# A fused attention and two-layer feed-forward kernel: float64 weights are loaded into their final places and converted in four stages, and two units share one product with v

## The chip, the cores and the metric

The kernel runs on one core of a Trainium2 chip. The metric is the device time of one execution in microseconds (us), as the median of several runs. Five engines work at once: TensorE (PE; its weight loads are shown apart as PEld), VectorE (DVE), ScalarE (ACT), GpSimd (POOL) and SyncE (SP), which issues most of the DMAs. Each engine runs its own instructions strictly in the order in which the program issues them, as the traces below show.

## The reference

Three layers follow each other, in float32 on activations; the four weight matrices arrive as float64 words:

```python
scores = q @ k.T / 8                     # 4 batches, 8 heads, 576 positions, head size 64
scores = where(mask, scores, -1e9)       # 4 heads: window of 32; 4 heads: 32 positions, 4 apart
x = softmax(scores) @ v                  # then 2304 tokens x 512
h = x @ w_in ; y = (h - tanh(h)) @ w_out           # 512 -> 2048 -> 512
h2 = y @ w_in2 ; s = h2 * softmax(h2)              # 512 -> 1024
out = layernorm(s) * g_ln @ w_out2                 # 1024 -> 512
```

## The kernel before, in words

The 2304 tokens form 6 groups of 384 (`G`). A group has 8 attention units (`NU`), 48 in all; a unit is two heads on two blocks of 96 queries with 128 keys each. Of a unit, `qk_f32` (units below 22) or `qk_half` makes the scores in PSUM and the DVE masks them and takes row minima (L163, L187, L190); `sm_exp` is the exponential on ACT (L198); `sm_norm` is two small DVE instructions (L203, L204) and one product on POOL (L205); `tr_pe` transposes on TensorE (L212) and ACT copies the result to `pt` (L218); `pv_pe` multiplies by v (L233), and ACT and DVE write the rounded part and the rest of the result into `x` (L243, L244). Units from 22 on need their operands in two parts as well, which `prep_unit` writes into `qks` with three DVE instructions (L139 to L142).

Products are made with float32r operands in two parts, high and rest, so that every product of the feed-forward layers takes three passes. A weight tile of 128 x 512 float64 words is loaded raw by `w_load` (L78, 512 KB), and `w_step` turns it into its two parts, one step of the pipeline for each of several tiles at once: ACT scales the upper words (L97), the DVE takes the sign and joins the parts of the word (L98, L101, L105), and two steps later ACT casts to the high part (L85) and the DVE subtracts it (L86).

The program has four stretches. **Start**: rounds r = 0 to 10 run the 8 units of the first group, and in rounds 1 to 10 one `w_step` each (`SW`). In a round TensorE has `qk(r)`, `pv(r - 3)`, `tr(r - 2)` in this order; the DVE has first the `w_step`, then the minima of unit r, the x part of an earlier unit and the norm of unit r - 1; ACT has its part of the `w_step`, then the exponentials of unit r and the copy to `pt`. SP issues, in order, the raw load of the `w_step`, then `load_unit(r + 3)`. **Main loop**: iteration s has two halves (slots). Half 0 is `mm1(s)`, 12 passes over one tile of `w_in` for group s // 16; half 1 is `mm2(s - 5)`, 12 passes over one tile of `w_out` that add to four PSUM tiles `yb`. `todo` holds the pieces of attention that TensorE does behind the passes of a slot, `later` the work of the other engines; `plan` lays them out by slot: unit u from 16 on starts in slot p = 4u - 41. In slots 0 to 41 `w_step` is called at the pace of WA steps in WB slots. After the 16th tile of a group `mm2` copies the four `yb` through an SBUF tile `ys` to `y_dr` in DRAM (L330, L331, L332), two at a time through one buffer. **Last group** (s from 80): no attention is left; one `w_step` per iteration converts `w_in2` and `w_out2` into the 16 places of `wi`, whose old tiles are used for the last time by `mm1(80)` to `mm1(95)`. **End**: for 18 tiles of 128 tokens `mm3`, `softmax`, `trz`, `mm4`, `store`.

Of the kernel before, what the change touches and what calls it, by code (L numbers as in the profile page):

```python
# [16 lines left out]
WIN, DIL = 32, 4  # L17
# [14 lines left out]
WA, WB = 24, 40  # L32
# [5 lines left out]
def tile_kernel(ctx: ExitStack, tc: tile.TileContext, qk, vw, cst, w_in, w_out, w_in2, w_out2, g_ln, out):  # L38
# [4 lines left out]
    wi_p = ctx.enter_context(tc.tile_pool(name="wi", bufs=NF, side="left"))  # L43
    wo_p = tc.alloc_tile_pool(name="wo", bufs=NF, side="left")
    raw_p = tc.alloc_tile_pool(name="raw", bufs=3, side="left")
    qs_p = None
# [25 lines left out]
    wq, wld, wa, wf = [], [], [], []  # L72
# [8 lines left out]
    def w_parts():  # L81
        if wf:
# [6 lines left out]
    def w_step():  # L89

        w_parts()
        new = wld.pop(0) if wld else None
        if new:
            lst, c, pool, tag, nm, r = new
            a = raw_p.tile([128, 512], F32, tag="wa", name="wa_" + nm, bufs=2)
            y = raw_p.tile([128, 512], I32, tag="wy", name="wy_" + nm, bufs=3)
            nc.scalar.activation(out=a, in_=r[:, :, 1].bitcast(F32), func=AF.Copy, scale=2.0 ** -112)  # L97
            nc.vector.tensor_scalar(out=y, in0=r[:, :, 1], scalar1=-2 ** 31, scalar2=None, op0=ALU.bitwise_and)  # L98
        if wa:
            *e, ao, yo = wa.pop(0)  # L100
            nc.vector.scalar_tensor_tensor(out=yo, in0=ao.bitcast(I32), scalar=3, in1=yo,  # L101
                                           op0=ALU.logical_shift_left, op1=ALU.bitwise_or)
            wf.append((*e, yo.bitcast(F32)))
        if new:
            nc.vector.scalar_tensor_tensor(out=y, in0=r[:, :, 0], scalar=29, in1=y,  # L105
                                           op0=ALU.logical_shift_right, op1=ALU.bitwise_or)
            wa.append((lst, c, pool, tag, nm, a, y))
# [4 lines left out]
    for c in range(NF + LAG):  # L112
        if c < NF:
            wq.append((wi, c, wi_p, w_in[c], "wi", f"wi{c}"))
        if c >= LAG:
            wq.append((wo, c - LAG, wo_p, w_out[c - LAG], "wo", f"wo{c - LAG}"))
# [6 lines left out]
    def load_unit(u):  # L123
        if u < NU * NG:
# [3 lines left out]
            v = at_p.tile([NK, 2, 2, D], F32, tag="v", name=f"v{u}", bufs=4)  # L128
# [3 lines left out]
    def prep_unit(u):  # L132
# [3 lines left out]
        s = qs_p.tile([128, QC + 2 * KC], F32R, tag="qks", name=f"qks{u}")  # L136
# [71 lines left out]
    def tr_pe(u, pool, tag, eng="a"):  # L208
# [4 lines left out]
        pt = at_p.tile([NK, QC], F32, tag="pt", name=f"pt{u}")  # L213
# [9 lines left out]
    def pv_pe(u, pool, tag):  # L223
        d = un.pop(u)
        g, r = divmod(u, NU)
        hp, bp = divmod(r, 2)
        if bp == 0:
# [408 lines left out]
```

## Time and profile before

| what | us |
|---|---|
| median of 3 runs (769.83 to 771.4) | 770.56 |
| the profiled execution, its own time | 771.82 |
| its span, first to last instruction | 770.0 |
| TensorE busy in it | 729.4 |

The profile shows one execution. An instruction has a start, a duration and, in brackets, the idle time of its engine before it with what ended that. Start times are us from the start of the span. Stretches of one engine's idle time matter only where the work that ends last waits for them. "Issue" as releaser means that the profile names no cause.

### The profile page before, as it was taken

The page shows a single profiled execution, that of the slowest core. Times are in us where ns is not written, and L with a number is a line of the kernel's source. Part 1 is how long each engine was busy: PE and PEld are TensorE (multiplying, and loading weights), DVE is VectorE, ACT ScalarE, POOL GpSimd, SP SyncE. Part 2 cuts the span into 40 slices and gives each one's busy share as a digit, 9 for nine tenths or more (in the row PEclk, how much of TensorE's full clock was granted, in tenths as well). Part 3 has the DMA queues.
Part 4 walks back from the last instruction along what each step waited for, and adds up shares of the span by engine and source line. Part 5 has one row for each costly group of instructions (what it writes and reads, how often), then busy time and mean ns, then how long its engine had stood idle before and what let it go on. Part 6 is the DMA issues. An engine that isn't in the chain of part 4 may idle for free.

```text
span 770.0 us, 11751 instructions
## 1 busy us (share of the span) xinstructions
PE 729.4 (95%) x4168; PEld 657.8 (85%) x4168; DVE 470.0 (61%) x1297; ACT 367.1 (48%) x1015; POOL 132.3 (17%) x187
## 2 busy tenths in 40 slices
PE   5658899999999999999999999799999999999998
PEld 4547789999999899989998999799888888888885
DVE  4688788746665766666666535498365555555453
ACT  4656666644443544444444434345145544445454
POOL 1210322111111111111111100010133123231210
PEclk9999899999999999999999999899999999999999
DMA  7565354222222222121212102434201011110001
GB/s 188 180 215 154 110 187 162 92 70 77 63 62 78 88 63 63 62 89 55 64 61 94 63 1 82 155 133 138 68 1 56 29 40 56 42 54 28 14 28 42
DMA packets 30283, 63.62 MB, mean 83 GB/s; under 512 B 3088, under 2 KB 16912, under 8 KB 30224
## 3 DMA queue, kind: packets, MB, share of 16 engines
q1 hardware_dynamic: 26960, 58.15, 23.6%
q10 hardware_dynamic: 3264, 4.72, 1.7%
q8 instruction: 33, 0.54, 0.3%
q14 instruction: 26, 0.21, 0.1%
HBM read 53.42 MB, written 9.44 MB: 82 GB/s over the span
## 4 chain that ended last, share of the span: by engine, by line
PE 88%; DMA 4%; DVE 3%; ACT 2%; issue 1%; POOL 1%; SPq 0%; ACTq 0%; POOLq 0%; DVEq 0%
PE y L325 27%; PE h L298 25%; PE po L529 13%; PE h L467 13%; PE pv L233 3%; PE zt L510 2%; DMA raw_wi<-in_w_in_dram 2%; PE qkp L158 2%; PE tp L212 2%; PE qkp L178 2%; ACT p L198 1%; DMA y_dr<-ys 1%; POOL p L205 1%; DVE wy_wi L105 1%; DMA raw_wo<-in_w_out_dram 0%
## 5 line engine op out<-in xcount | busy, mean ns | idle before, releaser
L298 PE MATMUL h<-x,wi 128*128 128x384 f32 x1152 | 225.3, 346 | 3.3 <-DVE x L244 2.0
L325 PE MATMUL y<-gs,wo 128*128 128x384 f32 x1152 | 222.6, 343 | 4.3 <-DVE ys L330 4.3
L325 PEld LDWEIGHTS y<-gs,wo 128*128 128x128 f32 x1152 | 199.9, 190 | 9.4 <-DVE ys L330 4.6
L298 PEld LDWEIGHTS h<-x,wi 128*128 128x128 f32 x1152 | 202.0, 193 | 5.5 <-DVE x L244 2.3
L205 POOL TENSOR_TENSOR p<-p,rs 96x512 f32<-96x512 f32 x48 | 77.9, 1623 | 368.0 <-DVE rs L204 315.3
L306 ACT ACTIVATE t<-h 128x384 f32<-128x384 f32 x96 | 46.9, 489 | 125.3 <-PE h L298 119.3
L467 PE MATMUL h<-w2i,yt 128*128 128x512 f32 x432 | 104.9, 397 | 0.0
L529 PE MATMUL po<-w2o,z 128*128 128x512 f32 x432 | 104.1, 396 | 0.1
L529 PEld LDWEIGHTS po<-w2o,z 128*128 128x128 f32 x432 | 80.7, 188 | 20.4 <-ACT z L518 1.9
L518 ACT ACTIVATE z<-zt,gl_sb 128x128 fp32r<-128x128 f32 x144 | 51.0, 367 | 96.9 <-PE zt L510 48.6
L467 PEld LDWEIGHTS h<-w2i,yt 128*128 128x128 f32 x432 | 79.7, 187 | 18.4
L198 ACT ACTIVATE p<-p,nm 96x128 f32<-96x128 f32 x192 | 75.0, 393 | 36.3 <-DVE nm L163 36.3
L519 DVE SCALAR_TENSOR_TENSOR z<-zt,gl_sb,z 128x128 fp32r<-128x128 f32 x144 | 48.9, 350 | 69.2 <-ACT z L518 69.2
L312 ACT CAST gs<-t 128x384 fp32r<-128x384 f32 x96 | 49.1, 511 | 54.0 <-DVE t L309 53.7
L244 DVE TENSOR_TENSOR x<-pv,x 128x192 fp32r<-128x192 f32 x48 | 20.5, 428 | 77.1 <-ACT x L243 77.1
L309 DVE TENSOR_TENSOR t<-h,t 128x384 f32<-128x384 f32 x96 | 52.9, 551 | 23.0 <-ACT t L306 22.9
L315 DVE TENSOR_TENSOR gs<-t,gs 128x384 fp32r<-128x384 f32 x96 | 56.1, 585 | 9.8 <-ACT gs L312 9.7
L233 PE MATMUL pv<-pt,v 128*64 128x96 f32 x384 | 29.7, 281 | 15.7 <-ACT pt L218 9.1
L233 PEld LDWEIGHTS pv<-pt,v 128*64 128x64 f32 x384 | 19.8, 151 | 28.6 <-issue 12.4
L158 PE MATMUL qkp<-qkr 64*96 64x128 f32 x176 | 31.6, 334 | 8.2 <-DMA qkr<-in_qk_dram 7.6
L387 POOL TENSOR_TENSOR yt<-yr,yt 128x1024 fp32r<-128x1024 f32 x9 | 21.9, 2430 | 93.9 <-DMA raw_w2o<-in_w_out_dram 62.3
L158 PEld LDWEIGHTS qkp<-qkr 64*96 64x96 f32 x176 | 25.9, 201 | 13.0 <-DMA qkr<-in_qk_dram 6.9
(68 smaller groups left out, 708.2 us busy)
## 6 DMA issues: line engine op xcount, KB each, us to landing
qkr<-in_qk_dram SPq DMA_DIRECT2D x26, 448.0 KB, 3.4
raw_wi<-in_w_in_dram SPq DMA_DIRECT2D x16, 512.0 KB, 4.5
raw_wo<-in_w_out_dram SPq DMA_DIRECT2D x16, 512.0 KB, 4.2
v<-in_vw_dram SPq DMA_DIRECT2D x48, 128.0 KB, 2.1
qkr<-in_qk_dram SPq DMA_DIRECT2D x22, 224.0 KB, 4.3
y_dr<-ys ACTq DMA_DIRECT2D x12, 384.0 KB, 2.4
yr<-y_dr SPq DMA_DIRECT2D x9, 512.0 KB, 4.1
out_dram<-o SPq DMA_DIRECT2D x18, 256.0 KB, 2.0
```

Source lines behind the costliest of these rows:

```text
L158: nc.tensor.matmul(ps[:, b], d["r"][:64, b * NQ:(b + 1) * NQ], d["r"][:64, QC + b * NK:QC + (b + 1) * NK], start=True, stop=True)
L198: nc.scalar.activation(out=d["p"][:, b], in_=d["p"][:, b], func=AF.Exp, scale=-1.0, bias=d["nm"][:, b:b + 1], accum_out=d["sm"][:, b:b + 1])
L205: nc.gpsimd.tensor_tensor(out=d["p"], in0=d["p"], in1=d["rs"].unsqueeze(2).to_broadcast([NQ, 4, NK]), op=ALU.mult)
L233: nc.tensor.matmul(ps[64 * h:64 * h + 64, b * NQ:(b + 1) * NQ], d["v"][:, b, h], d["pt"][:, (2 * h + b) * NQ:(2 * h + b + 1) * NQ], start= ...
L298: nc.tensor.matmul(ps, w[:, a, k * 128:(k + 1) * 128], xt[g, k][:, b], start=(n == 0), stop=(n == 3 * KD - 1))
L309: nc.vector.tensor_tensor(out=t, in0=ps, in1=t, op=ALU.subtract)
L312: nc.scalar.copy(out=gs[:, 0], in_=t)
L315: nc.vector.tensor_tensor(out=gs[:, 1], in0=t, in1=gs[:, 0].bitcast(F32), op=ALU.subtract)
L325: nc.tensor.matmul(yb[g][m], wo[c][:, a, m * 128:(m + 1) * 128], gs[:, b], start=(c == 0 and i == 0), stop=(c == NF - 1 and i == 2))
L467: nc.tensor.matmul(ps[:, n * 512:(n + 1) * 512], y[:, a, k, o:o + TT], w2i[2 * k + n][:, b], start=(q == 0), stop=(q == 3 * KD - 1))
L518: nc.scalar.activation(out=z[:, 0, c], in_=pp[n][:, j], func=AF.Copy, scale=gc)
L529: nc.tensor.matmul(po, z[:, a, j], w2o[j][:, b], start=(q == 0), stop=(q == 3 * NF2 - 1))
```

## The change

- Raw tiles have no pool of their own: each raw tile is loaded into the place that its two parts take later (tags `wi0` to `wi15`, `wo0` to `wo15`, one buffer each); scratch tiles for the conversion (`cv`) are kept for the whole program. Four raw tiles are loaded ahead in the start, where it was two.
- `w_step` has four stages: the DVE's subtraction (L86 before) comes one step after ACT's cast (L85), and stands first in the step; ACT's scaling stands ahead of the cast.
- WA is 26, where it was 24.
- `pv_pe` does two units in a row into one PSUM bank, with one pair of instructions for x; in the start it runs in rounds 4, 6, 8 and 10, in the main loop for odd u. `v` has 6 buffers for 4, `pt` 3 for 2.
- `qks` has one buffer for two, and its three instructions come in slots p + 2, p + 3, p + 3 where they came in p, p + 1, p + 2.
- `ys` holds all four tiles of a group, which go out with one DMA.

```diff
-WA, WB = 24, 40
+WA, WB = 26, 40
...
-            raw = raw_p.tile([128, 1024], I32, tag="raw", name="raw_" + nm)
+            raw = pool.tile([128, 1024], I32, tag=tag, name="raw_" + nm)
             nc.sync.dma_start(out=raw, in_=src)
...
     def w_step():
-        w_parts()
+        if wh:
+            lst, c, w, f = wh.pop(0)
+            nc.vector.tensor_tensor(out=w[:, 1], in0=f, in1=w[:, 0].bitcast(F32), op=ALU.subtract)
+            lst[c] = w
...
+            nc.scalar.activation(out=a, in_=r[:, :, 1].bitcast(F32), func=AF.Copy, scale=2.0 ** -112)
+            nc.vector.tensor_scalar(out=y, in0=r[:, :, 1], scalar1=-2 ** 31, scalar2=None, op0=ALU.bitwise_and)
         if wf:
             lst, c, pool, tag, nm, f = wf.pop(0)
             w = pool.tile([128, 2, 512], F32R, tag=tag, name=nm)
             nc.scalar.copy(out=w[:, 0], in_=f)
-            nc.vector.tensor_tensor(out=w[:, 1], in0=f, in1=w[:, 0].bitcast(F32), op=ALU.subtract)
-            lst[c] = w
+            wh.append((lst, c, w, f))
...
     def pv_pe(u, pool, tag):
+        ps = pool.tile([128, 512], F32, tag=tag, name=f"pv{u}")[:, 0:G]
+        for i in range(2):
+            d = un.pop(u + i)
+            for b in range(2):
+                for h in range(2):
+                    nc.tensor.matmul(ps[64 * h:64 * h + 64, (2 * i + b) * NQ:(2 * i + b + 1) * NQ], d["v"][:, b, h],
+                                     d["pt"][:, (2 * h + b) * NQ:(2 * h + b + 1) * NQ], start=True, stop=True)
...
     load_unit(2)
-    w_load()
+    for _ in range(3):
+        w_load()
...
-        b1 = pv_pe(r - 3, st_ps, "pv") if 0 <= r - 3 < NU else None
+        b1 = pv_pe(r - 4, st_ps, "pv") if r % 2 == 0 and 0 <= r - 4 < NU else None
...
-            for i in range(0, KD, 2):
-                ys = g_p.tile([128, 2, G], F32, tag="ys", name=f"ys{g}_{i}", bufs=1)
-                nc.vector.tensor_copy(out=ys[:, 0], in_=yb[g][i])
-                nc.scalar.copy(out=ys[:, 1], in_=yb[g][i + 1])
-                nc.scalar.dma_start(out=y_dr[:, i:i + 2, g * G:(g + 1) * G], in_=ys)
+            ys = g_p.tile([128, KD, G], F32, tag="ys", name=f"ys{g}", bufs=1)
+            for m in range(KD):
+                if m % 2 == 0:
+                    nc.vector.tensor_copy(out=ys[:, m], in_=yb[g][m])
+                else:
+                    nc.scalar.copy(out=ys[:, m], in_=yb[g][m])
+            nc.scalar.dma_start(out=y_dr[:, :, g * G:(g + 1) * G], in_=ys)
...
-                at(p, lambda u=u: preps.extend(prep_unit(u + 1)))
-                for i in range(3):
+                at(p + 2, lambda u=u: preps.extend(prep_unit(u + 1)))
+                for i in (2, 3, 3):
                     at(p + i, lambda: preps.pop(0)() if preps else None)
...
-            if u0 <= u - 2 < u1:
-                piece(q + 1, lambda u=u: pv_pe(u - 2, a_ps, "at"))
+            if u % 2 and u0 <= u - 3 < u1:
+                piece(q + 1, lambda u=u: pv_pe(u - 3, a_ps, "at"))
```

## Rows read from the trace of the kernel before

**Rows 1.** The page: busy time, share of span and instructions of each engine.
```profile
PE 729.4 (95%) x4168; PEld 657.8 (85%) x4168; DVE 470.0 (61%) x1297; ACT 367.1 (48%) x1015; POOL 132.3 (17%) x187
```
**Rows 2.** Waits of TensorE, whole span: total us, times, longest us.
```profile
PE pv L233 <- ACT pt L218: 9.1, 6, 3.5
...
PE y L325 <- DVE ys L330: 4.3, 1, 4.3
PE pv L233 <- issue: 3.8, 3, 1.3
```
**Rows 3.** Stage windows: busy us (instructions) by engine, granted clock, DMA share, GB/s.
```profile
450.00:500.00 50.00, 45.74 (x256) 44.69 (x256) 23.19 (x45) 18.14 (x37) 0.00 (x0) 0.93 0.27 90
```
**Rows 4.** Timeline, one round of the start: start, duration, engine, line, operation.
```profile
16.66 0.62 ACT L85 CAST wi<-wy_wi 128x512 fp32r<-128x512 f32 x1
...
16.80 0.91 PE L233 MATMUL pv<-pt,v 128*64 128x96 f32 x8 [0.35 <-ACT pt L218]
17.30 0.69 DVE L86 TENSOR_TENSOR wi<-wy_wi,wi 128x512 fp32r<-128x512 f32 x1 [1.74 <-ACT wi L85]
...
17.64 0.90 PE L212 MATMUL tp<-cst_sb,p 96*128 96x96 f32 x4
...
18.47 2.02 PE L158 MATMUL qkp<-qkr 64*96 64x128 f32 x8
...
19.45 0.28 DVE L163 CUSTOM_DVE_ANT_0 p<-qkp,cst_sb 96x128 f32<-96x128 f32 x1
...
20.49 0.17 DVE L204 RECIPROCAL rs<-rs 96x4 f32<-96x4 f32 x1
...
21.75 0.62 ACT L85 CAST wi<-wy_wi 128x512 fp32r<-128x512 f32 x1
```
**Rows 5.** Timeline, end of the start: minima of unit 7, first product.
```profile
40.25 0.28 DVE L163 CUSTOM_DVE_ANT_0 p<-qkp,cst_sb 96x128 f32<-96x128 f32 x1
...
52.88 6.67 PE L298 MATMUL h<-x,wi 128*128 128x384 f32 x24 [2.03 <-DVE x L244]
```
**Rows 6.** Stage window in the first loads, columns as in Rows 3.
```profile
8.00:12.00 4.00, 2.36 (x12) 2.04 (x12) 2.21 (x12) 2.38 (x11) 0.26 (x1) 1.00 0.97 274
```
**Rows 7.** Timeline, POOL: the same product in the start and later.
```profile
20.81 1.04 POOL L205 TENSOR_TENSOR p<-p,rs 96x512 f32<-96x512 f32 x1 [4.06 <-ACT p L198]
...
76.49 2.85 POOL L205 TENSOR_TENSOR p<-p,rs 96x512 f32<-96x512 f32 x1 [8.21 <-DVE rs L204]
```
**Rows 8.** Waits between 53 and 112 us, columns as in Rows 2.
```profile
DVE wi L86 <- ACT wi L85: 4.7, 4, 1.2
...
PE tp L212 <- POOL p L205: 4.2, 1, 4.2
```
**Rows 9.** Timeline of TensorE in the main loop, around one pv piece.
```profile
239.28 2.33 PE L298 MATMUL h<-x,wi 128*128 128x384 f32 x12
241.54 0.55 PE L233 MATMUL pv<-pt,v 128*64 128x96 f32 x8
242.02 2.36 PE L325 MATMUL y<-gs,wo 128*128 128x384 f32 x12
244.22 0.40 PE L178 MATMUL qkp<-qks 128*96 128x256 f32 x2
```
**Rows 10.** Timeline of the DVE at the end of group 1.
```profile
251.09 0.56 DVE L330 COPY ys<-y 128x384 f32<-128x384 f32 x1 [3.04 <-DMA y_dr<-ys]
```
**Rows 11.** Timeline of TensorE at the end of group 4.
```profile
480.44 2.24 PE L298 MATMUL h<-x,wi 128*128 128x384 f32 x12
...
484.60 2.24 PE L298 MATMUL h<-x,wi 128*128 128x384 f32 x12
...
492.14 2.29 PE L325 MATMUL y<-gs,wo 128*128 128x384 f32 x6 [4.26 <-DVE ys L330]
...
500.18 2.07 PE L298 MATMUL h<-x,wi 128*128 128x384 f32 x11
```
**Rows 12.** Loads of raw_w2i, the tile's view: from issue to landing.
```profile
DMA to landing us min/median/max: 3.0/3.2/4.4
```

More of the change, by code (lines that the diff above doesn't have):

```diff
@@ L42, in tile_kernel @@
     const = ctx.enter_context(tc.tile_pool(name="const", bufs=1, side="left"))
[L43 to L46, printed above, removed]
+    cv_p = ctx.enter_context(tc.tile_pool(name="cv", bufs=2, side="left"))
+    wi_p = ctx.enter_context(tc.tile_pool(name="wi", bufs=1, side="left"))
+    wo_p = tc.alloc_tile_pool(name="wo", bufs=1, side="left")
     g_p = ctx.enter_context(tc.tile_pool(name="g", bufs=2, side="right"))
@@ L85, in w_parts @@
             nc.scalar.copy(out=w[:, 0], in_=f)
[L86 to L98 removed]
+            wh.append((lst, c, w, f))
         if wa:
[L100 removed]
+            *eo, ao, yo = wa.pop(0)
             nc.vector.scalar_tensor_tensor(out=yo, in0=ao.bitcast(I32), scalar=3, in1=yo,
                                            op0=ALU.logical_shift_left, op1=ALU.bitwise_or)
[L103 removed]
+            wf.append((*eo, yo.bitcast(F32)))
         if new:
@@ L135, in prep_unit @@
         r = un[u]["r"]
-        s = qs_p.tile([128, QC + 2 * KC], F32R, tag="qks", name=f"qks{u}")
+        s = at_p.tile([128, QC + 2 * KC], F32R, tag="qks", name=f"qks{u}", bufs=1)
         un[u]["s"] = s
@@ L223, in pv_pe @@
     def pv_pe(u, pool, tag):
[L224 removed]
         g, r = divmod(u, NU)
[L226 to L240 removed]
+        hp = r // 2
+        x = xt[g, hp] = x_p.tile([128, 2, G], F32R, tag=f"x{hp}", name=f"x{g}_{hp}")
+        ps = pool.tile([128, 512], F32, tag=tag, name=f"pv{u}")[:, 0:G]
[5 more added lines that the diff above has]
+                                     d["pt"][:, (2 * h + b) * NQ:(2 * h + b + 1) * NQ], start=True, stop=True)
+        sl, src = [x[:, i] for i in range(2)], ps
+        if hp >= 2:
+            sl = [a.rearrange("p (i r) -> p r i", r=DIL) for a in sl]
+            src = ps.rearrange("p (r i) -> p r i", r=DIL)
         def then():
@@ L371, in tile_kernel @@
     w2i, w2o = [None] * (2 * KD), [None] * NF2
-    wq2 = [(w2i, 2 * k + n, wi_p, w_in2[k, n], "wi", f"w2i{2 * k + n}") for k in range(KD) for n in range(2)]
-    wq2 += [(w2o, j, wi_p, w_out2[j], "wi", f"w2o{j}") for j in range(NF2)]
+    wq2 = [(w2i, 2 * k + n, wi_p, w_in2[k, n], f"wi{2 * k + n}", f"w2i{2 * k + n}")
+           for k in range(KD) for n in range(2)]
+    wq2 += [(w2o, j, wi_p, w_out2[j], f"wi{2 * KD + j}", f"w2o{j}") for j in range(NF2)]
     yt, y_raw = {}, {}
@@ L396, in tile_kernel @@
     for s in range(NS + LAG):
-        if s == NF + LAG:
-            assert not (wq or wld or wa or wf)
-            raw_p.release()
-            qs_p = tc.alloc_tile_pool(name="qs", bufs=2, side="left", reuse_waits="tile")
         if s == NS - NF:
-            assert not todo and not later and not (wq or wld or wa or wf), (todo, later)
+            assert not todo and not later and not (wq or wld or wa or wf or wh), (todo, later)
             a_ps.release()
             at_p.release()
-            qs_p.release()
-            raw_p = tc.alloc_tile_pool(name="raw2", bufs=2, side="left", reuse_waits="tile")
             h2a = tc.alloc_tile_pool(name="h2a", bufs=1, space=PSUM, side="right", reuse_waits="tile")
```

35 lines of the change are left out of this document (13 added, 22 removed).

## The prediction

> **What bounds the kernel now.** The page comes first: TensorE is busy for 95% of the span [rows 1]. In such a kernel only TensorE's idle time, its time at the lower clock and work taken from it can be won, so the second view is the list of TensorE's waits [rows 2]. It names three that this change touches: pv waits for the copy to pt (9.1 us, in the start), y waits once for a copy to ys (4.3 us), and pv waits three times 1.3 us for "issue". The third view, busy time by stage, adds the clock: between 450 and 500 us, where the wait for ys lies, the granted clock is 0.93 on average [rows 3]. In the start the clock reads full, but there the same pv piece takes 0.91 us and in the main loop 0.55 us [rows 4, 9], so the start runs near the lower level of 1.2 GHz. The end of the kernel is not touched; it keeps its time.
>
> **The start: the ring of a round.** Followed back by its releasers, a round is a ring of ACT and DVE: ACT's cast at 16.66, the DVE's subtraction that waited for it at 17.30, the rest of the step on the DVE, the minima at 19.45, the exponentials and the pt copy on ACT, and behind them the next cast at 21.75: 5.1 us [rows 4]. From unit 3 (19.45) to unit 7 (40.25) the minima come 20.8 us apart, 5.2 us a round [rows 4, 5]. The four-stage step opens the ring: the subtraction uses a cast of the step before, so the DVE waits for no cast of its own round. What is left is the next longest of the engines. The DVE needs 3.36 us from the subtraction to the reciprocal's end (17.30 to 20.66) and some 0.25 us for x: 3.6 us. TensorE at the lower clock needs 2.0 for qk, 0.84 for pv and 0.83 for the transposes (starts at 16.80, 17.64, 18.47): 3.7 us. I take 3.9 us, because POOL's product, which fell into the DVE's wait, now collides with the DVE (below). Four rounds: 20.8 - 15.6 = 5.2 us won.
>
> Two things take from this. Four raw tiles instead of two are queued before the units' own loads; the DMA engines are full then, 274 GB/s at a share of 0.97 [rows 6], so two more tiles of 0.52 MB hold the operands of unit 3 back by 2 x 1.9 us. Unit 3 had nearly that much slack, its minima waiting for the DVE; I charge 0.25 us, with 0 to 2 as bounds. A round moves 0.88 MB (units 0.22 + 0.13, raw 0.52), 3.2 us at that rate, below 3.9.
>
> The tail from unit 7's minima to the first product takes 12.63 us now [rows 5]. Behind the change it is this chain: minima, x and a norm 1.7 us; a step 2.15 (17.30 to 19.45); the norm of unit 7 0.36; the next step 2.15, in which POOL is shut out, then its product 1.04; transposes 0.9 and copy 0.4; pv of two units 1.8; both parts of x 1.05: 11.6 us, 1.0 won. Together the start wins 5.2 - 0.25 + 1.0 = 6.0 us; bounds 2 and 9 (the upper one if the denser work brings TensorE to 2.4 GHz and POOL is not held).
>
> POOL's product takes 1.04 us in the start, beside a DVE that waits, and 2.85 us later, beside one that works [rows 7]; that is the collision that I charge. The Trainium skill, "SBUF — State Buffer", section "SBUF: two separate sides", says that the DVE and GpSimd share a pair of ports as an exclusive lock held for a whole instruction, by DVE instructions with two SBUF inputs among others. By it the fast rows of the start hold only as long as the DVE idles there. By the row of the start alone, the tail would be 10.4 us and a round 3.7, and the whole sum 2.0 us more.
>
> **The first slots of the main loop.** Here the DVE is late: TensorE waits 4.2 us for POOL's product of one unit, which waits for the norm on the DVE, and the DVE's subtraction waits four times for the cast, 4.7 us [rows 8]. Two of these waits stand ahead of that norm. WA = 26 moves no more steps ahead of it: slots 0, 1, 3, 4, 6, 8 have one before, 0, 1, 3, 4, 6, 7 behind. So TensorE goes on by 1.2 to 2.4 us earlier, and the first pv leaves this stretch at the lower clock (0.91) and comes back at the full one (0.5). I take 2.0 us; bounds 0 (the step in slot 7 delays the minima of unit 9 as much) and 4 (the clock does not fall).
>
> **pv of two units in a row.** In the main loop TensorE has no gap, so its own time counts. Two plain products of 12 passes take 4.16 us (480.44 to 484.60), 2.08 each [rows 11]. The product ahead of a pv piece takes 2.26 (239.28 to 241.54), the piece 0.48, the product behind it 2.20 [rows 9]: a piece costs 0.78, of which 0.30 is entry and exit. A second unit in the same piece pays 0.48 again and no second entry. 20 pairs in the main loop: 20 x 0.30 = 6.0 us. From below the bound is 0, if the second unit's first weights pay the entry again; above, 6.5.
>
> The Trainium skill, "TensorE: Matmul & The Clock Gate", section "Part 2: What happens when you issue a matmul", says that TensorE pulls weight loads ahead of matmuls in flight when their rows do not conflict, or into a background buffer. Taken alone, that would leave no entry to save and this term at 0; the row shows 0.18 us at the entry. The result by it stands among the rivals.
>
> **ys with four tiles.** Now the second pair of copies waits for the first DMA, 3.04 us at the end of group 1 [rows 10]; the DVE stands still, the PSUM buffer of a piece stays full, and the next pv has its wait for "issue", three times, 3.8 us [rows 2]. At the end of group 4 the copy waits longer, and product y with it: 4.26 us, and the clock drops. From the product at 484.60 to the one two iterations later at 500.18 are 15.58 us, where two iterations take 8.32: 7.26 us lost [rows 11]. With four tiles no copy waits for a DMA of its own group; the DMA before it is a whole group old. The last copy ends half a microsecond behind the product, and nobody needs the bank before the next `mm2`. Won: 3.8 + 7.3 = 11.1 us; lower bound 8.1, if a part of the clock's fall comes back.
>
> **What I cost at nothing.** Weights are ready one step later; the pace pays for it (`wi[15]` needs step 28, 30 are done; `wo[10]` step 29, 31 are done). The raw loads of `w_in2` and `w_out2` get a new wait: place k is free only behind `mm1(80 + k)`. Queued behind it on SP are the later raw loads and the loads of y; ACT's scaling and the DVE's step of the next iteration wait for it, and behind these the rest of tanh's work. A load lands in 3.2 us, at most 4.4 [rows 12]; then scaling, cast, high part and tanh(s + 1) on ACT and the DVE's subtraction end some 2.8 us later (five instructions of 0.5 to 0.6), 6.0 to 7.2 us behind `mm1(s)`. The PSUM buffer that this frees is wanted by `mm1(s + 3)`, five products or 10.4 us behind it. The cover is 3 to 4 us; if it is gone, each of 16 iterations grows by the excess. `qks` with one buffer: the first of three DVE instructions comes a slot behind the last reader, and they end a slot before TensorE needs them; cover some 3 us. Longer v and pt chains wait on older buffers only.
>
> **Sum.** 6.0 + 2.0 + 6.0 + 11.1 = 25.1 us. The profiled execution's own time of 771.82 becomes 746.7; it lies 1.3 above the median, so the median becomes 745.5, rounded 746.
>
> **Rivals.** (1) The loads rule the start: the operands of unit 3 come 2 us late and rounds stay at 4.8 us, so that the start wins 0.6 instead of 6.0: 751. For it speaks the full DMA [rows 6], against it that four prefetched tiles leave the queue only the mean rate to keep. (2) A pair pays its entry twice: 752. (3) The new wait of the raw loads spreads: beside the y loads they land after 8 us, beyond the cover, and 16 iterations grow by 0.5 to 1 us: 754 to 762. (4) Slower: the single `qks` stops TensorE in each of 25 units, because the DVE is late with it by more than its cover of 3 us. From 1.0 us a unit on, the whole gain of 25.1 us is gone; at 1.5 us the time is 783. Against it speaks that the DVE is idle for 39% of the span [rows 1]. (5) The chain of the ys copies just moves: the loads of y and the single larger DMA let TensorE wait as before, and 7.3 us are not won: 753.
>
> **How the numbers follow.** Forecast 0.60; rivals: (1) 0.13, (2) 0.12, (3) 0.04, (4) 0.04, (5) 0.04; several of them at once 0.03, of which 0.02 would end within 0.2%. All upper bounds of the terms at once win 5.5 us more, half of the way to all lower bounds loses 7.5 us: 740 to 753. The range of 739 to 756 adds (1), (2), (5) and part of (3), and leaves out (4) and the ends. Changes below 0.2%, 1.5 us, can't be told from none here. Faster 0.94, same 0.02, slower 0.04.
>
> **What would show it.** In the profile behind the change: minima of units 3 to 7 some 3.9 us apart and the first product near 47 us; no wait of y for ys and no pv that waits for "issue"; a pv piece of 16 matmuls near 0.96 us with one entry; clock 1.0 between 450 and 500 us; ACT and the DVE idle for raw_w2i once an iteration without a wait of TensorE. A first product later than 50 us, a second entry inside a pair, or TensorE waiting for qks would make the prediction wrong.

## The result, and the profile after

| | before | after |
|---|---|---|
| median of the runs (lowest to highest) | 770.47 us (769.83 to 771.4) | 746.64 us (746.35 to 747.18) |
| the profiled execution, its own time | 771.82 | 747.18 |
| its span | 770.0 | 745.4 |
| TensorE busy in it | 729.4 | 717.0 |

The ratio is 0.9691, with a 95% interval of 0.9674 to 0.9707: 23.8 us are won, where 25.1 were forecast. The first view of after is again the list of TensorE's waits (total, times, longest, in us).

```profile
PE qkp L158 <- DMA qkr<-in_qk_dram: 11.2, 4, 4.4
PE tp L212 <- POOL p L205: 5.4, 6, 2.3
PE qkp L158 <- DVE nm L163: 3.8, 2, 3.6
PE h L297 <- DVE x L242: 1.8, 1, 1.8
PE qkp L178 <- DVE qks L142: 0.8, 3, 0.3
```

The three waits of [rows 2] are gone, down to one of 0.5 us for pv. What stands there now lies mostly in the start and the first slots: operands from DRAM, GpSimd's product, the minima. Only the `qks` line, three small waits, belongs to the main loop.

The timeline of after gives the landmarks of the start: the minima of units 3 and 7, and the first product.

```profile
20.17 0.29 DVE L163 CUSTOM_DVE_ANT_0 p<-qkp,cst_sb 96x128 f32<-96x128 f32 x1 [2.32 <-PE qkp L158]
...
35.21 0.29 DVE L163 CUSTOM_DVE_ANT_0 p<-qkp,cst_sb 96x128 f32<-96x128 f32 x1 [0.70 <-PE qkp L158]
...
47.42 6.69 PE L297 MATMUL h<-x,wi 128*128 128x384 f32 x24 [1.83 <-DVE x L242]
```

Four rounds take 15.04 us, 3.76 each, against 20.8 in [rows 4, 5]. In the first slots behind it one wait is left, and the matmuls behind it run at the lower clock (4.04 us for 12 passes):

```profile
67.23 2.02 PE L158 MATMUL qkp<-qkr 64*96 64x128 f32 x8 [3.62 <-DVE nm L163]
69.17 4.04 PE L297 MATMUL h<-x,wi 128*128 128x384 f32 x12
```

In the main loop a piece holds both units' products with v, 16 matmuls:

```profile
228.07 2.33 PE L297 MATMUL h<-x,wi 128*128 128x384 f32 x12
230.33 0.88 PE L233 MATMUL pv<-pt,v 128*64 128x96 f32 x16
231.14 2.35 PE L324 MATMUL y<-gs,wo 128*128 128x384 f32 x12
...
308.08 0.88 PE L233 MATMUL pv<-pt,v 128*64 128x96 f32 x16
327.88 0.88 PE L233 MATMUL pv<-pt,v 128*64 128x96 f32 x16
```

The window from 450 to 500 us, where [rows 3] had a busy time of 45.74 and a clock of 0.93, has no gap at all now:

```profile
450.00:500.00 50.00, 50.00 (x290) 50.00 (x289) 39.09 (x72) 23.85 (x48) 4.65 (x1) 1.00 0.50 164
```

Two more landmarks are the DVE's first copy to `ys` and the first `mm3`, here before and after:

```profile
167.82 0.56 DVE L330 COPY ys<-y 128x384 f32<-128x384 f32 x1 [1.88 <-PE y L325]
...
548.02 11.36 PE L467 MATMUL h<-w2i,yt 128*128 128x512 f32 x48
```

```profile
158.53 0.56 DVE L330 COPY ys<-y 128x384 f32<-128x384 f32 x1 [1.88 <-PE y L324]
...
522.94 11.36 PE L462 MATMUL h<-w2i,yt 128*128 128x512 f32 x48
```

Set side by side, the landmarks say where the time went. The first product comes 5.46 us earlier (52.88 to 47.42), the DVE's first copy to `ys` 9.29 (167.82 to 158.53), the first `mm3` 25.08 (548.02 to 522.94). The end, which the change leaves alone, takes 222.5 us instead of 222.0, so that the span is 24.6 us shorter. The medians differ by 23.8 because the profiled execution of before lies 1.35 us above its median, that of after 0.54.

### The profile page after: what moved, and what is told of

Same layout as the page of the kernel before. It is cut to its first block, busy times and chain, and to the rows that moved or that the text cites. A ratio compares the mean times of both kernels' runs of the same rounds, so it can differ in the third digit from the quotient of the medians.

```text
span 745.4 us, 11617 instructions
## 1 busy us (share of the span) xinstructions
PE 717.0 (96%) x4168; PEld 653.4 (88%) x4168; DVE 490.8 (66%) x1273; ACT 365.5 (49%) x991; POOL 134.7 (18%) x187
## 4 chain that ended last, share of the span: by engine, by line
PE 88%; DVE 5%; ACT 3%; DMA 2%; POOL 1%; issue 1%; ACTq 0%; SPq 0%; POOLq 0%; DVEq 0%
PE y L324 26%; PE h L297 24%; PE po L524 14%; PE h L462 14%; PE qkp L158 3%; PE pv L233 2%; PE zt L505 2%; PE tp L212 2%; DMA qkr<-in_qk_dram 2%; PE qkp L178 2%; ACT p L198 1%; POOL p L205 1%; DVE gs L314 1%; DVE wi L85 1%; DVE p L163 1%
## 5 line engine op out<-in xcount | busy, mean ns | idle before, releaser
L324 PE MATMUL y<-gs,wo 128*128 128x384 f32 x1152 | 217.3, 338 | 0.0
L314 DVE TENSOR_TENSOR gs<-t,gs 128x384 fp32r<-128x384 f32 x96 | 75.7, 788 | 20.9 <-ACT gs L311 18.8
L158 PE MATMUL qkp<-qkr 64*96 64x128 f32 x176 | 32.5, 340 | 15.6 <-DMA qkr<-in_qk_dram 11.2
L242 DVE TENSOR_TENSOR x<-pv,x 128x384 fp32r<-128x384 f32 x24 | 16.9, 703 | 40.0 <-ACT x L241 40.0
L389 POOL TENSOR_TENSOR yt<-yr,yt 128x1024 fp32r<-128x1024 f32 x9 | 24.3, 2697 | 85.8 <-DVE yt L388 85.8
L479 DVE SCALAR_TENSOR_TENSOR u<-h,e 128x1024 f32<-128x1024 f32 x18 | 22.0, 1225 | 23.9 <-ACT e L478 23.9
L198 ACT ACTIVATION_READ_ACCUMULATOR p<-p,nm 96x1 f32 x192 | 36.2, 188 | 0.0
```

The source lines that it names most:

```text
L158: nc.tensor.matmul(ps[:, b], d["r"][:64, b * NQ:(b + 1) * NQ], d["r"][:64, QC + b * NK:QC + (b + 1) * NK], start=True, stop=True)
L198: nc.scalar.activation(out=d["p"][:, b], in_=d["p"][:, b], func=AF.Exp, scale=-1.0, bias=d["nm"][:, b:b + 1], accum_out=d["sm"][:, b:b + 1])
L314: nc.vector.tensor_tensor(out=gs[:, 1], in0=t, in1=gs[:, 0].bitcast(F32), op=ALU.subtract)
L324: nc.tensor.matmul(yb[g][m], wo[c][:, a, m * 128:(m + 1) * 128], gs[:, b], start=(c == 0 and i == 0), stop=(c == NF - 1 and i == 2))
```

## The experiments

All kernels were timed against the kernel before on the same chip. Unless another is named, each starts from the changed kernel and alters one thing. Prices are differences of medians to the 746.64 us above. The kernel before came out at 769.26 to 771.29 us in the four comparisons, so a difference of 1 us across two of them shows nothing. No run takes back by itself the pace WA, the pairs of the start, the places of the raw tiles or the single `qks` buffer.

### Undoing one part at a time

**Cast and subtraction in one step again.** ACT's cast is moved from the third stage to just ahead of the DVE's subtraction, as in the kernel before.

```diff
+        if wf:
+            lst, c, pool, tag, nm, f = wf.pop(0)
+            w = pool.tile([128, 2, 512], F32R, tag=tag, name=nm)
+            nc.scalar.copy(out=w[:, 0], in_=f)
+            wh.append((lst, c, w, f))
         if wh:
             lst, c, w, f = wh.pop(0)
...
-        if wf:
...
```

> The changed kernel with one thing undone: the DVE's subtraction stands again in the step of ACT's cast, behind it; loads, places, pace and pairs stay as changed. Theory (the ring of ACT and DVE set the round): minima of units 3 to 7 again some 5.1 us apart instead of 3.8, the first product at 52 to 53 us instead of 47.4, a time of 752 to 754 us. Rival (the loads ahead and the separate places shortened the start): rounds stay below 4.2 us, the first product before 49 us, a time below 748.5 us.

754.85 us (754.37 to 755.37), 8.2 above the changed kernel and a little above the 752 to 754 expected. Its DVE timeline shows the ring again: the subtraction waits 1.74 us for the cast, and the minima of successive units come 5.1 us apart.

```profile
23.16 0.69 DVE L90 TENSOR_TENSOR wi<-wy_wi,wi 128x512 fp32r<-128x512 f32 x1 [1.73 <-ACT wi L86]
...
25.31 0.28 DVE L163 CUSTOM_DVE_ANT_0 p<-qkp,cst_sb 96x128 f32<-96x128 f32 x1
...
28.25 0.69 DVE L90 TENSOR_TENSOR wi<-wy_wi,wi 128x512 fp32r<-128x512 f32 x1 [1.74 <-ACT wi L86]
...
30.40 0.28 DVE L163 CUSTOM_DVE_ANT_0 p<-qkp,cst_sb 96x128 f32<-96x128 f32 x1
```

The first product is at 52.74, back at the place of [rows 5] (52.88) although four tiles are still loaded ahead and pv still goes in pairs. So without the fourth stage nothing of the gain in the start is left. The stretch from the first product to the first copy of `ys` grows as well, from 111.1 to 113.6 us: 2.5 us of the first slots hang on the same wait.

**One unit per piece in the main loop.** `pv_one` is `pv_pe` of the kernel before; the start keeps its pairs.

```diff
-            if u % 2 and u0 <= u - 3 < u1:
-                piece(q + 1, lambda u=u: pv_pe(u - 3, a_ps, "at"))
+            if u0 <= u - 2 < u1:
+                piece(q + 1, lambda u=u: pv_one(u - 2, a_ps, "at"))
```

> The changed kernel with pv done unit by unit in the main loop, as before; the start keeps its pairs. Theory (a pair pays entry and exit of a pv piece once): 20 pairs lose 0.3 to 0.4 us each, 752.6 to 754.6 us, and two units take 19.7 us on TensorE in the main loop instead of 19.3. Rival (the pair costs TensorE what two single pieces cost): 746 to 747.5 us.

752.77 us (752.37 to 752.89), 6.1 more: 0.31 us for each of 20 pairs. TensorE's timeline has a piece every 9.85 us:

```profile
223.63 0.55 PE L233 MATMUL pv<-pt,v 128*64 128x96 f32 x8
...
233.48 0.55 PE L233 MATMUL pv<-pt,v 128*64 128x96 f32 x8
```

Two units take 19.70 us here and 19.32 in the changed kernel, 0.38 less. Between the landmarks the price is smaller: from the first product to the first `mm3` this execution takes 480.66 us, two executions of the changed kernel 475.52 and 475.05. The list of waits of this kernel has no `qks` line, though `qks` has one buffer here too.

**Two tiles of `ys` at a time again**, the code of the kernel before in `mm2`.

```diff
-            ys = g_p.tile([128, KD, G], F32, tag="ys", name=f"ys{g}", bufs=1)
...
+            for i in range(0, KD, 2):
+                ys = g_p.tile([128, 2, G], F32, tag="ys", name=f"ys{g}_{i}", bufs=1)
...
```

> The changed kernel with ys for two tiles and two DMAs per group through one buffer, as before. Theory (both kinds of waits at group ends came from ys): three waits of 1.3 us at the ends of groups 1 to 3 and 4.3 us with the fall of the clock at the end of group 4 come back, 757 to 758 us. Rival (the pairs already removed the three short waits, since behind the end of a group there is no pv piece any more in the next slot): only 7.3 us come back, 753.5 to 754.5 us, and TensorE has one wait for ys in its list.

758.64 us (757.98 to 759.1), 12.0 more. The waits are back, at two places (list of waits):

```profile
PE qkp L178 <- DVE qks L142: 6.8, 3, 2.3
...
PE y L324 <- DVE ys L329: 1.9, 1, 1.9
```

The DVE stands 3.02 us in front of the second copy, for the first DMA, as in [rows 10]. But TensorE now pays for it in the scores, not in pv: with one buffer, `qks` is late by 2.3 us at the end of a group. In the kernel before the same delay cost 1.3 us each [rows 2]. The wait is not all of it: behind two of the three waits the clock falls (granted 0.57 from 244 to 248 us). From one pv piece to the next the three ends of groups take 23.34, 23.39 and 21.79 us where other pairs take 19.32, 10.6 us in all; in the kernel before they took 11.2 us where other pieces take 9.86, 4.0 in all. At the end of group 4 it is the other way round: the wait of y is 1.9 us here against 4.26 in [rows 11], and from the last pv piece to the first `mm3` this kernel loses 3.75 us against the changed one (83.71 to 79.96), where [rows 11] lost 7.3. The time lies near the theory's 757 to 758, but its parts are others.

The three prices add up to 26.3 us, 2.5 more than the whole change wins. They are not shares of the gain: with the single `qks` buffer, two tiles of `ys` cost 6.5 us more at the ends of groups than in the kernel before, and 3.5 us less at the end of group 4.

### The wait that the change brought in the first slots

**The steps of the main loop later by 9/26 of a slot** (the expectations call it a quarter), so that the step of slot 7 falls into slot 8 and no longer stands ahead of unit 9's minima.

```diff
-            if s < NF + LAG and done[0] < W0 + WA * (slot + 1) // WB or s > NS - NF and half == 0:
+            if s < NF + LAG and done[0] < W0 + (WA * (slot + 1) - 9) // WB or s > NS - NF and half == 0:
```

> The changed kernel with the pace of the weight steps shifted, so that a step that fell into slot 7 of the main loop falls into slot 8, behind the minima of unit 9. Theory (that step is what makes TensorE wait 3.6 us for these minima, and the wait brings the lower clock for the next two pieces): the wait falls below 1.5 us, the clock stays at 1.0 between 60 and 75 us, a time of 741 to 743.5 us. Rival (the DVE has too much to do in these slots wherever the step stands): the wait comes back one or two slots later, 745.5 to 747.5 us.

745.93 us (745.35 to 746.37), a ratio of 0.9689 against 0.9691: no difference that can be told. TensorE's timeline shows why.

```profile
65.84 1.11 PE L158 MATMUL qkp<-qkr 64*96 64x128 f32 x8 [1.47 <-DVE nm L163]
66.89 3.75 PE L297 MATMUL h<-x,wi 128*128 128x384 f32 x12
...
72.33 0.55 PE L212 MATMUL tp<-cst_sb,p 96*128 96x96 f32 x4 [1.69 <-POOL p L205]
```

The wait for the minima shrinks from 3.62 to 1.47 us, and a wait of 1.69 us for the next unit's norm appears, by way of GpSimd. The clock does not stay at 1.0 as the theory had it: the product behind the shorter wait takes 3.75 us, and 0.87 is granted from 60 to 70 us. The DVE is busy for 9.88 of these 10 us. Moving its work by a slot renames a good part of the wait, but not all: from the first product to the first copy of `ys` this execution takes 109.01 us, two executions of the changed kernel 111.11 and 110.72. In the time, the later first product (48.19) hides some of these 2 us.

### GpSimd's product, the loads and the tail of the start

The start of the same code does not repeat exactly: in five executions with the changed kernel's start the first product came at 46.18, 47.42, 47.58, 47.79 and 48.19 us, and the minima of unit 3 between 18.88 and 20.22. A shift below 1 us at that place shows nothing by itself. The tail behind the minima of unit 7 repeats: 12.20 or 12.21 us in all five.

**The norm ahead of the minima**, in the start.

```diff
+        if r >= NU and r - 1 < NU:
+            sm_norm(r - 1)
         if r in SW:
             w_step()
+        if 0 <= r - 1 < NU - 1:
+            sm_norm(r - 1)
         if t:
             t()
...
-        if 0 <= r - 1 < NU:
-            sm_norm(r - 1)
```

> The changed kernel with one order altered in the start: on the DVE, the norm of unit r-1 (1e-9 added, reciprocal) stands ahead of the minima of unit r instead of behind them, and for the last unit ahead of the step. In the changed kernel GpSimd's product takes 2.85 us in six of the eight rounds of the start, beside the step's subtraction and its bit operations on the DVE; in the kernel before it took 1.04, beside a DVE that waited. Theory (the step's instructions hold GpSimd back): a product that begins ahead of the minima has them and the DVE's wait for TensorE beside it, so most products fall to 1.0 to 1.6 us, TensorE's waits for GpSimd in the start (1.39 and 2.35 us at 39.96 and 43.21) shrink to less than half, the first product comes 1.5 to 2.5 us earlier (45 to 46 instead of 47.4), and the time is about 744.5. Rival (the length comes from something else, such as GpSimd's own start or the full DMA): the products stay at 2.85 us, the norm waits for the exponentials and delays the minima, a round grows from 3.76 to 4 us or more, and the time is 747 to 749.

745.5 us (745.24 to 746.61), ratio 0.9668 (0.9654 to 0.9683). GpSimd's timelines, first of the changed kernel, then of this one:

```profile
29.31 2.85 POOL L205 TENSOR_TENSOR p<-p,rs 96x512 f32<-96x512 f32 x1 [1.66 <-ACT p L198]
32.56 2.85 POOL L205 TENSOR_TENSOR p<-p,rs 96x512 f32<-96x512 f32 x1 [0.41 <-ACT p L198]
```

```profile
30.40 1.04 POOL L205 TENSOR_TENSOR p<-p,rs 96x512 f32<-96x512 f32 x1 [3.39 <-DVE rs L204]
33.98 1.03 POOL L205 TENSOR_TENSOR p<-p,rs 96x512 f32<-96x512 f32 x1 [2.54 <-DVE rs L204]
36.41 4.99 POOL L205 TENSOR_TENSOR p<-p,rs 96x512 f32<-96x512 f32 x1 [1.40 <-DVE rs L204]
```

Seven products fall to 1.04 us. The eighth, which now begins beside the first instruction of a step and has a second step right behind that one, takes 4.99 us. It ends 0.98 us after the DVE has turned to an x that it reads from PSUM (40.42):

```profile
36.16 0.66 DVE L85 TENSOR_TENSOR wi<-wy_wi,wi 128x512 fp32r<-128x512 f32 x1
36.74 0.42 DVE L93 TENSOR_SCALAR wy_wi<-raw_wi 128x512 int32<-128x512 int32 x1
...
39.82 0.68 DVE L105 SCALAR_TENSOR_TENSOR wy_wo<-raw_wo,wy_wo 128x512 int32<-128x512 int32 x1
40.42 0.84 DVE L242 TENSOR_TENSOR x<-pv,x 128x384 fp32r<-128x384 f32 x1
```

The length was the DVE's doing: the theory holds on that. On the time it does not: a round shrinks only from 3.76 to 3.72 us (3.77 to 4.01 in the four other executions of the unchanged start) and the tail from 12.21 to 11.92, and the intervals of the two ratios overlap. The first product comes at 45.65, as expected, but one execution of the unchanged start had it at 46.18. GpSimd was hardly on the path of a round.

**Two raw tiles ahead instead of four.**

```diff
-    for _ in range(3):
-        w_load()
+    w_load()
```

> The changed kernel with two raw tiles loaded ahead of the units' own loads instead of four, as in the kernel before. In the changed kernel TensorE waits for the operands of unit 3 until 18.04 us, and the first minima that follow the new pace are at 20.17, 0.7 later than the same ones in the kernel before (19.45); the charge for this in the prediction was 0.25 us, with 0 to 2 as bounds. Theory (the two extra tiles of 0.52 MB stand ahead of these operands in the queue, at 1.9 us each): the operands come 2 to 3.5 us earlier, the minima of unit 3 near 18.5, and the first product 0.5 to 1.5 us earlier, because the later steps then wait for their raw tiles for a part of it: 745 to 746. Rival (the DMA engines are full whatever the order, and what is taken from the operands goes to the steps): the steps wait for their raw tiles from the second on, rounds grow from 3.76 to over 4 us, and the first product comes at 47.5 to 50: 747 to 749.

745.84 us (745.12 to 746.38), ratio 0.9671 (0.9654 to 0.9687). The minima of unit 3 come at 18.46 as expected, those of unit 7 at 34.09, 3.91 us a round, and the first product at 45.96. Of 1.7 us at unit 3 against the changed kernel's profile, 1.1 are left at unit 7. But one of the five executions with four tiles had these minima at 18.88, so that the two tiles cost between 0.4 and 1.8 us there, and in the time nothing can be told from it.

**The last two products on the DVE.**

```diff
-        nc.gpsimd.tensor_tensor(out=d["p"], in0=d["p"],
+        (nc.vector if u in (NU - 2, NU - 1) else nc.gpsimd).tensor_tensor(out=d["p"], in0=d["p"],
```

> The changed kernel with the normalizing product of units 6 and 7 on the DVE instead of GpSimd; the other units stay. It measures what the tail of the start pays for GpSimd being held: in the changed kernel the tail from the minima of unit 7 to the first product takes 12.21 us, where 11.6 were charged with 1.04 us for this product and 10.4 was the figure without any holding. Theory (TensorE's two waits for GpSimd, 1.39 and 2.35 us, lie on the chain that sets the first product): the product takes some 0.7 us on the DVE, the transposes of unit 7 start near 41 instead of 43.21, and the first product comes 1.8 to 2.5 us earlier, near 45.2, a tail of 10.0 to 10.4; the time is about 744.5. Rival (the DVE sets the chain anyway, as its queue holds both parts of x and two steps): the first product comes less than 0.7 us earlier and the time stays at 746 to 747.

746.42 us (746.06 to 747.38), ratio 0.968 (0.9665 to 0.9694). The theory falls: the tail is 11.41 us (34.98 to 46.39), not 10.0 to 10.4. The first product comes 1.0 us earlier than in the changed kernel's profile, between theory and rival, and the time is the rival's. TensorE gets its transposes sooner and then waits longer for x, 3.35 us instead of 1.83:

```profile
46.39 7.08 PE L297 MATMUL h<-x,wi 128*128 128x384 f32 x24 [3.35 <-DVE x L242]
```

### Three edits at once, and what bounds the first 80 us

**The norm ahead of the minima, two tiles ahead, the steps of the main loop later**, all three.

> The changed kernel with three edits of earlier runs at once: the norm ahead of the minima in the start, two raw tiles loaded ahead instead of four, and every step of the main loop a quarter of a slot later. Alone they moved the span by -2.0, -1.6 and -1.4 us. Theory (up to some 80 us the DVE is the bound, so what one edit wins ahead of it is partly given back as a wait for minima or norms there): the first product comes near 44.5 us, the first copies of ys no more than 3 us earlier than in the changed kernel, and the time is 743 to 744.5, 2 to 3.5 us below it. Rival (the gains simply add, being in different waits): 5.0 us, 741.5. Rival on the other side (later raw loads and later steps meet, and products wait for weights): 746 or more.

743.1 us (742.6 to 743.59), ratio 0.9659 (0.9642 to 0.9677). The first product comes at 45.12, the first copy of `ys` 3.4 us earlier than in the run of the changed kernel beside it, where the theory allowed 3. The time falls within the theory's range, 3.5 us below 746.56. It does not decide against the rival: the gains that it adds up to 5.0 us are spans of single executions, and by medians the three edits alone lie 1.1, 0.8 and 0.7 us below 746.64, 2.6 in all.

**The same, and the product of unit 7 on the DVE.**

> The kernel with the three edits, and the normalizing product of unit 7 on the DVE instead of GpSimd. With the norm ahead of the step GpSimd's last product ran beside two steps and took 4.99 us, and TensorE waited 3.53 us for it. Theory (that wait lies on the chain to the first product): the product takes 0.7 us, the transposes of unit 7 start 3 us earlier or more, and what is late next is the DVE, with three steps and two x in its queue; the first product comes 1 to 2.5 us earlier than with the three edits alone, the time 0.5 to 2 us earlier. Rival (the DVE's queue sets the first product in any case): within 0.5 us of the three edits alone.

742.52 us (741.16 to 743.42), ratio 0.9647 (0.9627 to 0.9666). The 3.5 us that TensorE waited for the 4.99 us product are gone, but the first product comes only 0.66 us earlier (44.46), because x is late instead. The times of this kernel and the one above overlap, so theory and rival stay undecided.

**The changed kernel itself** in the same comparison.

> The changed kernel itself, beside the two above on the same chip, so that differences of 1 to 3 us can be told: 746 to 747.2.

746.56 us (745.17 to 747.71), ratio 0.9703 (0.9684 to 0.9723). The two kernels above are faster than the changed one by 3.5 and 4.0 us; their intervals lie wholly below this one.

**The tenth step behind x**, from the kernel with unit 7 on the DVE.

```diff
-        if r in SW:
+        if r in SW and r != NU + 2:
             w_step()
...
     back()
+    w_step()
```

> The kernel with the three edits and unit 7's product on the DVE, with the tenth step of the start put behind both parts of the last pair's x instead of ahead of them. In that kernel TensorE waits 3.16 us for this x, which the DVE could start at 42.2 (when ACT's part ends) and starts at 43.57. The DVE does the same work in all. Theory (from the start to some 80 us the DVE's work in all is the bound): the first product comes 1 to 1.5 us earlier, near 43.2, but the seventh (72.55 there is the sixth listed) at most 0.5 us earlier, and the time stays within 0.7 us of 742.5. Rival (the chain to the first product sets what follows): the later products keep the 1 to 1.5 us, and the time is 741 to 741.5.

743.2 us (742.65 to 744.76), ratio 0.9652 (0.9637 to 0.9666). The first product comes 1.0 us earlier than with the step ahead of x, and the step that was passed over is paid one product later, in the wait for the DVE's part of tanh:

```profile
43.45 6.59 PE L299 MATMUL h<-x,wi 128*128 128x384 f32 x24 [1.81 <-DVE x L242]
...
54.92 2.35 PE L299 MATMUL h<-x,wi 128*128 128x384 f32 x12 [1.55 <-DVE t L310]
```

The first copy of `ys` is at 154.53, against 154.31 without this edit. The theory holds in what it forecast: the earlier first product gains nothing behind. That the DVE's work in all sets the time is argued from this and from its busy time (63.6 of the 70 us from 10 to 80); no run takes work from the DVE.

**The steps later still**, by a slot and a half instead of a quarter, from the kernel just above (`WA * (slot + 1) - 40`, where it was 9).

> The kernel with the last step behind x, and the steps of the main loop a slot and a half later than by the changed kernel's pace instead of a quarter of a slot, so that one step less (2.2 to 2.4 us of the DVE) stands ahead of the norms and minima of units 8 to 10. Theory (there TensorE waits for the DVE's work in all, 1.47 us for minima and 3.12 for the norm by way of GpSimd): these waits shrink by 1.5 to 2.4 us together, and the time falls by as much, to 740 to 741.2. Rival (the wait only moves to the next unit, because the step comes one slot later ahead of that unit's norm): no more than 0.5 us.

742.76 us (742.08 to 743.39), ratio 0.9641 (0.9628 to 0.9655). The theory's time does not come: the norm's wait of 3.1 us falls to 0.45, the wait for the minima grows from 1.47 to 3.61, two waits of 0.96 and 0.62 us are new at 84.29 and 87.55, and the first copy of `ys` is at 154.52, the same place. But the edit does not do all that was expected of it. Ahead of the minima of units 8 and 10 stands one step less, ahead of unit 9's as many as without it: the steps of slots 1, 3, 4, 6 and 7 instead of 0, 1, 3, 4 and 6. So the step of slot 7 is back, and with it the changed kernel's wait of 3.6 us and the lower clock (3.92 us for the 12 passes behind it). What one step less would give is not shown.

## Why the prediction was right, and which terms were off

**The start, 6.0 forecast, 5.46 measured** (4.7 to 6.7 over the five executions of this start, against one of the kernel before). The step that carried it, that the ring of cast, subtraction, minima and exponentials sets the round and that a fourth stage opens it, is shown by the kernel with cast and subtraction together. By terms: the rounds gained more than charged, 5.76 us for 5.2, because the 3.9 us a round held a charge for GpSimd's collision that the round hardly pays (3.76 with it, 3.72 without). The delay of unit 3 was mis-sized: its minima come 0.72 us later than in [rows 4] (20.17 to 19.45), charged with 0.25. And the tail takes 12.21 us, not 11.6. The sum is 5.76 - 0.72 + 0.42 = 5.46. Only the tail is firm: in the five executions the minima of unit 3 come at 18.88 to 20.22 and a round takes 3.76 to 4.01 us, so the forecast of 3.9 and part of the charge lie within the scatter. The remark that the sum would be 2.0 us more without the collision failed: the collision was there in six of eight rounds, and taking it away won 0.04 us a round, and 0.8 in the tail where the DVE took over the last two products. The tail is the DVE's queue of steps and x, as the kernels with products on the DVE show; in each one the wait for GpSimd becomes in part a wait for x.

**The first slots, 2.0 forecast, 2.3 to 2.9 measured** (114.94 us from the first product to the first copy of `ys` before, 111.11 after; 2.3 if four pairs won 4 x 0.38 of it, 2.9 by the kernel with single pieces, which takes 112.08). The reason given was half right. The two waits for the cast are gone, and the kernel with cast and rest together loses 2.5 us here. But the lower bound named the step in slot 7 ahead of unit 9's minima, and that came: 3.62 us of waiting, and the lower clock behind it. Both happened. What the prediction did not see is the bound behind the waits: the DVE has little room in these slots (busy 27.6 of the 30 us from 50 to 80), so the removed wait of 4.2 us [rows 8] turned into this one. Of the later edits of the order, the step moved behind unit 9's minima won some 2 us of this stretch; the others moved the waits on.

**Pairs, 6.0 forecast.** A pair saves 0.38 us, not 0.30: the piece takes 0.81 from its start to the next product's (230.33 to 231.14), and two single ones took 2 x 0.48 and two entries. The second unit costs 0.33, less than the 0.48 that was charged again. Entry and exit cost less than the prediction's 0.30 as well: a product behind transposes takes 2.16 us with no pv piece behind it (238.24 to 240.40, below), so 0.08 of the 0.18 that was read as entry in [rows 9] belongs to the transposes ahead. A single piece then costs 0.70, a pair 1.02. 20 x 0.38 = 7.6 us, if the four pairs of the first slots, where TensorE waits anyway, gave as much as the others (1.0 instead of 1.5 by the kernel with single pieces). The Trainium skill, "TensorE: Matmul & The Clock Gate", section "Part 2: What happens when you issue a matmul", has weight loads pulled ahead of matmuls in flight, from which the prediction had worked out that, taken alone, nothing would be saved; 0.38 us a pair stands against that for these pieces with 64 columns of weights.

**`qks`, forecast at nothing.** Here the step failed, by a small sum. The cover of "some 3 us" is right inside a group. At the ends of groups 1 to 3 the DVE copies `ys` first, and the last instruction for `qks` is late:

```profile
237.96 0.49 PE L212 MATMUL tp<-cst_sb,p 96*128 96x96 f32 x4
238.24 2.33 PE L297 MATMUL h<-x,wi 128*128 128x384 f32 x12
240.40 2.24 PE L324 MATMUL y<-gs,wo 128*128 128x384 f32 x12
242.90 0.45 PE L178 MATMUL qkp<-qks 128*96 128x256 f32 x2 [0.26 <-DVE qks L142]
```

The shown wait is 0.26 us, the loss 0.48: a pair around a group's end takes 19.80 us (308.08 to 327.88), the others between 172 and 425 us 19.32. Three times 0.48 are 1.4 us, so that pairs and `qks` together give 6.2, and the kernel with single pieces, which has no wait for `qks`, is 6.1 us slower (5.1 to 5.6 between the landmarks). The term of 6.0 came out about right by two errors of opposite sign, which is luck. The prediction had named TensorE waiting for `qks` as a sign that it is wrong; the sign is there, with 0.8 us in the list of waits. The kernel with two tiles of `ys` shows what the single buffer costs where the DVE is late by 3 us: waits of 2.3 us each, and 2.5 to 4.1 us each with what the clock adds.

**`ys`, 11.1 forecast.** What the other terms leave of 25.08 us at the first `mm3` is 25.08 - 5.46 - 2.3 - 6.2 = 11.1 us. That is a remainder. The rows of before bear it out: 4.0 us at the ends of groups 1 to 3 and 7.3 at the end of group 4, and after the change no wait of y for `ys` and none of pv for "issue" is in the list. The kernel with two tiles is 12.0 us slower, but loses 10.6 and 3.75 us at these places, with `qks` in part: it shows that the waits come from the two tiles, not how large the term was in the kernel before. That the lost clock would come back in full was right: 1.00 between 450 and 500 us.

**What was costed at nothing and stayed so.** The raw loads of `w_in2` land after 3.1 to 5.2 us (median 3.3), a little later than [rows 12], and ACT waits for them 16.3 us and the DVE 8.8 in all; TensorE has no wait for it. The third rival (the wait of the raw loads spreads) did not happen.

```profile
  ACT wa_w2i L92: 16.3, 6
  DVE wy_w2i L93: 8.8, 6
...
DMA to landing us min/median/max: 3.1/3.3/5.2
```

**Rivals.** The first one (operands of unit 3 late, rounds at 4.8 us) came true in its first half, up to 1.8 us late by the kernel with two tiles ahead, and not in its second: the rounds took 3.76 to 4.01 us. The second (a pair pays its entry twice) falls with the 0.38 us a pair saves, the fifth (the chain of the `ys` copies just moves) with the list of waits. The fourth (single `qks`) was right about the mechanism and wrong about the place: three ends of groups, not 25 units.

## What to carry to other kernels

Where a round is a ring through two engines, one more pipeline stage that lets each engine use the other's result of the round before takes the ring apart; the price to look for is what the deeper prefetch holds back. When an engine is nearly full over a stretch (the DVE here, busy 61.4 of the 70 us from 10 to 80), a named wait can be removed and come back under another name: test it by moving a piece of its work and looking at a landmark far behind, not at the next wait. A buffer that is halved because its cover is long enough in the steady state is to be checked at the boundaries, where the same engine does something else first; and copies out of PSUM that share one small buffer cost most where the next stage needs that bank.

## What the runs showed of the hardware that was not expected

**The DVE and GpSimd hold each other up, and the order of starting decides.** GpSimd's product takes 1.04 us when the DVE idles or reads PSUM, 2.85 when it begins beside the first instruction of a step and 4.99 when a second step follows without a gap: it gets nothing between the instructions of the steps. A missing gap is not all that counts, though. In the changed kernel the small norm instruction right behind a step waited for the product, 1.00 us where it takes 0.16 otherwise (timeline of all engines; the same in five other runs with this order):

```profile
37.06 2.85 POOL L205 TENSOR_TENSOR p<-p,rs 96x512 f32<-96x512 f32 x1 [1.65 <-DVE rs L204]
...
38.93 1.00 DVE L203 TENSOR_SCALAR rs<-sm 96x4 f32<-96x4 f32 x1
```

Why this instruction gave way and those of the steps did not is open. GpSimd holds up the DVE's larger instructions too. The DVE's busy time rose from 470.0 to 490.8 us though it has 24 instructions fewer, and 19.6 us of that are one line, the second part of tanh's result: its mean went from 585 to 788 ns. In the changed kernel GpSimd's product begins just ahead of it in 29 units, from 140 us on (timelines of GpSimd and the DVE):

```profile
281.30 1.04 POOL L205 TENSOR_TENSOR p<-p,rs 96x512 f32<-96x512 f32 x1 [7.26 <-DVE rs L204]
```

```profile
281.44 1.32 DVE L314 TENSOR_TENSOR gs<-t,gs 128x384 fp32r<-128x384 f32 x1 [0.30 <-ACT gs L311]
```

Otherwise the instruction takes 0.55 us; in the kernel before only four of the 96 took 1.32. There a `qks` instruction stood between the norm and this subtraction; GpSimd's product began beside it (294.71), was kept out until the subtraction behind it had ended too, and took 1.71 us, the subtraction 0.55. The 20 us cost no time, since TensorE does not wait for it. The Trainium skill, "SBUF — State Buffer", section "SBUF: two separate sides", tells of this lock and that whichever starts first has it for its whole instruction; 1.32 against 0.55 us agrees. That the two steps in a row keep GpSimd out until they end is what the 4.99 us add.

**The clock does not always fall behind the same wait.** Behind a wait of 3.62 us at 67.23 the changed kernel ran the scores (2.02 us) and the product (4.04 us for 12 passes) at the lower level of 1.2 GHz; 0.80 was granted from 60 to 70 us. In the second profile of the same kernel the scores behind the wait of 3.60 us took 1.11 us, the figure at full clock, and the clock fell only in the product, with 0.90 granted from 60 to 70:

```profile
67.05 1.11 PE L158 MATMUL qkp<-qkr 64*96 64x128 f32 x8 [3.60 <-DVE nm L163]
68.09 3.89 PE L297 MATMUL h<-x,wi 128*128 128x384 f32 x12
```

The stretch to the first copy of `ys` differs by 0.4 us between the two (111.11 to 110.72). In the kernel with two tiles of `ys`, waits of 2.25, 2.30 and 2.26 us for `qks` were followed by products of 3.58, 3.10 and 2.24 us: the clock fell twice and held once, in one execution. And behind 1.47 us for unit 9's minima the product took 3.75 us with the steps later alone, 2.35 with the three edits and unit 7 on the DVE. Why is open.
